# An MLP stage in sweeps of two column groups, with seven block products in place of eight for two token blocks

## The chip, the cores and the metric

One core of one Trainium2 chip runs the whole kernel. The metric is the time of the kernel on the device in microseconds (us), the median of several executions. A trace of one more execution, taken by the hardware profiler, is the source of every row shown. Engines have short names: PE is TensorE (matrix products), PEld its weight loads, DVE is VectorE, ACT is ScalarE, POOL is GpSimd, SP issues the DMAs.

## The reference

```python
attn = linear_attention(q, k, v, omega)          # 4 batches, 8 heads, 576 tokens, head size 64
x = attn.reshape(2304, 512)
xn = x / sqrt(mean(x * x) + 1e-6) * rms_g
x = (silu(xn @ w_gate) * (xn @ w_val)) @ w_out   # 512 -> 1536 -> 512, the GLU stage
out = silu(x @ w_in) @ w_out2                    # 512 -> 2048 -> 512, the MLP stage
```

The weights arrive in 64-bit floats. The result has 2304 x 512 elements in 32-bit floats.

## The kernel before

Tokens lie in five blocks j = 0 to 4 of 512, 512, 512, 512 and 256 tokens. A block's activations `xs[j]` are held with the 512 features in four chunks of 128 partitions, split in two parts, a high part and a low part (what the high part leaves over). Weights are split in the same way. A product of two such operands is three matmuls for each chunk (`PASS`: high by high, high by low, low by high).

The GLU and the MLP stage run in **sweeps**. A sweep holds the weights of a few groups f of 128 hidden columns in SBUF and goes over all blocks with them. The MLP stage has 16 groups, in six sweeps of 3, 3, 3, 3, 2 and 2. Sweeps alternate between two sets of weight slots: side 0 is `w0_0` to `w0_5`, side 1 is `w1_0` to `w1_8`. Slots 0 to 2 of side 1 lie in a pool of their own (`we`). A sweep's input weights "i" come in the first slots, its output weights "p" in the next ones.

For a block j and a group f, `g1_mlp` (L254) makes the input product in an accumulator of tag `g` (12 matmuls through `part`, L226), ACT takes the SiLU (L260) into a tile of tag `s`, and `split_h` (L217) makes the two parts of h: ACT copies the high part (L219), DVE subtracts (L220). When all groups of the sweep are done for a block, `g2_mlp` (L300) makes the output products in accumulators of tag `y`, one for each 128 tokens, with three matmuls a group (L313). DVE adds each into the block's sum `ya[j]` (L324). In the first MLP sweep ACT copies instead (L322), in the last the sums are stored by DMA. Tags `g` and `y` have four accumulators each, `s` has three tiles, `h` four.

`g2_mlp` is a generator. It is put into the program in the middle of the next block's work (`pend`, passed as `mid` or `late`), so that PE has an input product to do while ACT and DVE finish h.

The weights of the next sweep are prepared by `Prep.tick` (L193), which the loop at the end of the kernel (L1031) calls whenever the costs given out by the generators (`yield`, in us of PE) have added up to over 5.5. One tick takes each weight in the pipe a step further: load (DMA of 512 KB), then decode (five DVE operations, L151, L154, L157, L159 and L162, and two POOL additions, L165), then the high part (ACT, L171), then the low part (DVE, L174).

Each engine runs its instructions in the order in which the program writes them. An instruction that waits holds up all that is behind it on its engine.

Of the kernel before, what the change touches and what calls it, by code (L numbers as in the profile page):

```python
# [8 lines left out]
F32 = mybir.dt.float32  # L9
F32R = mybir.dt.float32r  # L10
# [10 lines left out]
def kernel(  # L21
# [14 lines left out]
    nc = tc.nc  # L36
# [48 lines left out]

    ident = const.tile([P, P], F32)
    make_identity(nc, ident)
    bd = const.tile([P, 2, 2 * P], F32R)
    g_sb = const.tile([P, DM], F32)
    mhalf = const.tile([P, 1], F32)  # L90

    xs = [big.tile([P, 2, KC, n], F32R, name=f"xs{j}") for j, n in enumerate(blocks)]
# [9 lines left out]
    sweeps = []  # L102
    f = 0
    for i, n in enumerate([2, 3, 2, 3, 2]):
        sweeps.append((1, list(range(f, f + n)), i % 2))
        f += n
    assert f == NF1
    f = 0
    for i, n in enumerate([3, 3, 3, 3, 2, 2]):
        sweeps.append((2, list(range(f, f + n)), (i + 1) % 2))  # L110
        f += n
    assert f == NF2
    wt = {}

    def wcols(w, f):
# [3 lines left out]
        return w.bitcast(U32)[f * P:(f + 1) * P, :]  # L119

    def prep_list(si):
        kind, fs, side = sweeps[si]
        if kind == 1:
            gv = [e for f in fs for e in (("g", f, wcols(w_gate, f)), ("v", f, wcols(w_val, f)))]
            if si == 0:
                gv.sort(key=lambda e: e[0])
            srcs = gv + [("o", f, wrows(w_out, f)) for f in fs]
        else:
            srcs = [("i", f, wcols(w2_in, f)) for f in fs] + [("p", f, wrows(w2_out, f)) for f in fs]
        return [(side, n, (kind, nm, f), ap) for n, (nm, f, ap) in enumerate(srcs)]  # L130

    class State:
        pass
# [31 lines left out]
            tt(out=mi, in0=mi, in1=(low if step == 5 else high).bitcast(I32), op=ALU.add)  # L165

    def w_high(job, st):
        side, slot, key, ap = job
        pool = pools["w"][2] if side and slot < W_EARLY else pools["w"][side]
        st.t = pool.tile([P, 2, KC * P], F32R, tag=f"w{side}_{slot}", name=f"w{side}_{slot}")  # L170
        nc.scalar.activation(out=st.t[:, 0, :], in_=st.m.bitcast(F32), func=AF.Copy)  # L171

    def w_low(job, st):
# [40 lines left out]
    W_EARLY, GRAIN = 3, 3  # L214
    W_PRIO, F_PRIO = 500.0, 1000.0

    def split_h(s, j):  # L217
        ht = pools["h"][0].tile([P, 2, blocks[j]], F32R, tag="h", name="h", bufs=pools["h"][1])
        nc.scalar.activation(out=ht[:, 0, :], in_=s, func=AF.Copy)  # L219
        nc.vector.tensor_tensor(out=ht[:, 1, :], in0=s, in1=ht[:, 0, :].bitcast(F32), op=ALU.subtract)  # L220
        return ht

    def part(w, j, ps, n0, n1):
        for n in range(n0, n1):
# [29 lines left out]
    def g1_mlp(f, j, hs, mid, late):  # L254
        prep.need((2, "i", f))
        p = ps_tile("ps_g", [P, blocks[j]])
        yield from proj(wt[2, "i", f], j, p)
        yield from late
        s = pools["s"][0].tile([P, blocks[j]], F32, tag="s", name="s", bufs=pools["s"][1])
        nc.scalar.activation(out=s, in_=p, func=AF.Silu)  # L260
        hs[f] = split_h(s, j)
        yield from mid

    def g2_glu(fs, j, hs, first, last):
# [10 lines left out]
        for d in range(KC):  # L275
            ps = ps_tile("ps_y", [P, blocks[j]])
            n = 0
            for f in fs:
                for a, c in PASS:
                    nc.tensor.matmul(  # L280
                        out=ps,
                        lhsT=wt[1, "o", f][:, a, d * P:(d + 1) * P],
                        rhs=hs[f][:, c, :],
                        start=(n == 0),
                        stop=(n == nn - 1),
                    )
                    n += 1
            if first:
                nc.scalar.activation(out=y[:, d, :], in_=ps, func=AF.Copy)
            else:  # L290
                nc.vector.tensor_tensor(out=y[:, d, :], in0=ps, in1=y[:, d, :], op=ALU.add)  # L291
            if last:
                nc.scalar.activation(out=xs[j][:, 0, d, :], in_=y[:, d, :], func=AF.Copy)
                if d:
                    low(d - 1)
            yield nn * blocks[j] / 2365
        if last:
# [32 lines left out]
    n1 = max(i for i, s in enumerate(sweeps) if s[0] == 1)  # L330
    n2 = len(sweeps) - 1

    def stream():
        pend = ()
        prepped = 1
        for si, (kind, fs, side) in enumerate(sweeps):
            for j in range(NB) if si < n2 else [*range(NE), *range(NB - 1, NE - 1, -1)]:
                if si == 0 and j < NE:
                    continue
                hs = {}  # L340
                end = si == n2 and j == NE
                for f in fs:
                    if kind == 1:
# [1 line left out]
                        pend = ()  # L345
                    else:
                        short = blocks[j] < TB * P
                        keep = f == fs[0] and (end or short)
                        mid, late_mid = ((), pend) if short else (pend, ())
                        yield from g1_mlp(f, j, hs, *(((), ()) if keep else (mid, late_mid)))  # L350
                        if not keep:
                            pend = ()
                    if si and prepped == si and si + 1 < len(sweeps):
                        prep.jobs += prep_list(si + 1)
                        prepped += 1
                if kind == 1:
                    pend = g2_glu(fs, j, hs, si == 0, si == n1)
                else:
                    pend = g2_mlp(fs, j, hs, si == n1 + 1, si == n2, end)
        yield from pend  # L360
# [607 lines left out]
    with tc.manual_schedule():  # L968
# [59 lines left out]
        pools["s"] = (late, 3)  # L1028
        prep.jobs += prep_list(1)[W_EARLY:]
        due = 0.0  # L1030
        for c in stream():  # L1031
            due += c
            if due > (W_PACE if prep.done(1) else W_RUSH):
                prep.tick()
# [31 lines left out]
```

## Time and profile before

| what | value |
|---|---|
| time, median of 3 runs | 1016.72 us (1016.62 to 1016.73) |
| time of the profiled execution | 1016.95 us |
| its span | 1015.2 us |
| PE busy | 1006.4 us (99%) |
| DVE busy | 582.5 us (57%) |
| ACT busy | 375.9 us (37%) |
| POOL busy | 282.7 us (28%) |

The span is the time from the first to the last instruction of the program. 1.75 us of the profiled execution lie outside it. Busy shares are means over stages of different kinds; the MLP stage runs from about 610 us to the end.

### The profile page before, as it was taken

The page shows a single profiled execution, that of the slowest core. Times are in us where ns is not written, and L with a number is a line of the kernel's source. Part 1 is how long each engine was busy: PE and PEld are TensorE (multiplying, and loading weights), DVE is VectorE, ACT ScalarE, POOL GpSimd, SP SyncE. Part 2 cuts the span into 40 slices and gives each one's busy share as a digit, 9 for nine tenths or more (in the row PEclk, how much of TensorE's full clock was granted, in tenths as well). Part 3 has the DMA queues.
Part 4 walks back from the last instruction along what each step waited for, and adds up shares of the span by engine and source line. Part 5 has one row for each costly group of instructions (what it writes and reads, how often), then busy time and mean ns, then how long its engine had stood idle before and what let it go on. Part 6 is the DMA issues. An engine that isn't in the chain of part 4 may idle for free.

```text
span 1015.2 us, 14341 instructions
## 1 busy us (share of the span) xinstructions
PE 1006.4 (99%) x5423; PEld 863.5 (85%) x5423; DVE 582.5 (57%) x1289; ACT 375.9 (37%) x861; POOL 282.7 (28%) x287
## 2 busy tenths in 40 slices
PE   8999999999999999999999999999999999999998
PEld 7999998888888888888888888888888888888887
DVE  6899999727852345676332775433654544535633
ACT  6888887344221112222112334443322322322312
POOL 7656653405520013344000331321411312201300
PEclk9999999999999999999999999999999999999999
DMA  7453312202320002232000120210210210200023
GB/s 184 105 151 95 84 43 64 63 21 83 104 62 1 1 1 64 67 98 64 21 1 1 42 63 22 83 42 15 69 42 14 70 43 21 63 1 21 21 84 104
DMA packets 68725, 55.78 MB, mean 55 GB/s; under 512 B 25648, under 2 KB 62768, under 8 KB 68656
## 3 DMA queue, kind: packets, MB, share of 16 engines
q1 hardware_dynamic: 68656, 54.87, 18.4%
q8 instruction: 43, 0.70, 0.3%
q14 instruction: 26, 0.21, 0.1%
HBM read 50.14 MB, written 4.72 MB: 54 GB/s over the span
## 4 chain that ended last, share of the span: by engine, by line
PE 95%; DVE 3%; DMA 1%; SPq 0%; issue 0%; ACT 0%; POOL 0%; DVEq 0%
PE g L226 44%; PE y L313 19%; PE y L280 12%; PE b L590 5%; PE kv L673 3%; PE b L226 3%; PE b L718 3%; PE b L945 2%; PE b L704 2%; PE b L571 1%; PE b L824 1%; DVE w L174 1%; DMA va<-in_v_dram 1%; DVE m L151 0%; DVE raw L154 0%
## 5 line engine op out<-in xcount | busy, mean ns | idle before, releaser
L226 PE MATMUL g<-xs,w 128*128 128x512 f32 (+1 forms) x2256 | 472.8, 368 | 0.0
L226 PEld LDWEIGHTS g<-xs,w 128*128 128x128 f32 x2256 | 391.8, 188 | 74.1
L165 POOL TENSOR_TENSOR m<-m,raw 128x512 int32<-128x512 int32 x136 | 190.6, 1401 | 619.1 <-issue 434.9
L220 DVE TENSOR_TENSOR h<-s,h 128x512 fp32r<-128x512 f32 (+1 forms) x134 | 95.5, 713 | 187.8 <-ACT h L219 187.8
L313 PE MATMUL y<-w,h 128*128 128x512 f32 (+1 forms) x870 | 201.6, 389 | 0.0
L313 PEld LDWEIGHTS y<-w,h 128*128 128x128 f32 x870 | 162.2, 188 | 34.1
L219 ACT ACTIVATE h<-s 128x512 fp32r<-128x512 f32 (+1 forms) x134 | 78.8, 588 | 192.5 <-DVE s L249 170.5
L280 PE MATMUL y<-h,w 128*128 128x512 f32 (+1 forms) x648 | 135.6, 366 | 0.1
L280 PEld LDWEIGHTS y<-h,w 128*128 128x128 f32 x648 | 112.1, 189 | 20.5 <-DVE w L174 0.5
L260 ACT ACTIVATE s<-g 128x512 f32<-128x512 f32 (+1 forms) x80 | 44.5, 556 | 174.5 <-PE g L226 174.3
L324 DVE TENSOR_TENSOR ya<-y,ya 128x512 f32<-128x512 f32 (+1 forms) x91 | 62.3, 684 | 58.6 <-PE y L313 57.5
L249 DVE TENSOR_TENSOR s<-s,g 128x512 f32<-128x512 f32 (+1 forms) x54 | 33.9, 627 | 90.1 <-PE g L226 90.1
L291 DVE TENSOR_TENSOR ya<-y,ya 128x512 f32<-128x512 f32 (+1 forms) x80 | 50.3, 635 | 55.1 <-PE y L280 54.8
L629 ACT ACTIVATE e<-b,nb 128x128 f32<-128x128 f32 x272 | 77.5, 386 | 9.0 <-DVE nb L618 8.6
L171 ACT ACTIVATE w<-m 128x512 fp32r<-128x512 f32 x68 | 42.7, 628 | 100.8 <-POOL m L165 100.7
L590 PE MATMUL b<-bd,hl 128*128 128x256 f32 x432 | 69.3, 297 | 0.3 <-DVE hl L580 0.2
L590 PEld LDWEIGHTS b<-bd,hl 128*128 128x128 f32 x432 | 56.4, 191 | 1.8 <-DVE hl L580 0.8
L243 ACT ACTIVATE s<-g 128x512 f32<-128x512 f32 (+1 forms) x54 | 29.7, 550 | 65.9 <-PE g L226 65.7
L174 DVE TENSOR_TENSOR w<-m,w 128x512 fp32r<-128x512 f32 x68 | 51.5, 758 | 4.1 <-ACT w L171 3.8
L605 DVE TENSOR_REDUCE small<-b 128x4 f32<-128x512 f32 x72 | 50.1, 696 | 5.9 <-PE b L590 3.3
L530 POOL TENSOR_TENSOR sq<-x 128x512 f32<-128x512 f32 (+1 forms) x40 | 39.4, 987 | 33.5 <-DVE rd L744 7.3
L534 POOL TENSOR_TENSOR sq<-sq 128x256 f32<-128x256 f32 (+2 forms) x80 | 44.7, 569 | 3.3
(69 smaller groups left out, 781.7 us busy)
## 6 DMA issues: line engine op xcount, KB each, us to landing
raw<-in_moe_w_out_dram SPq DMA_DIRECT2D x28, 512.0 KB, 3.5
raw<-in_moe_w_in_dram SPq DMA_DIRECT2D x16, 512.0 KB, 3.6
raw<-in_moe_w_gate_dram SPq DMA_DIRECT2D x12, 512.0 KB, 3.5
raw<-in_moe_w_val_dram SPq DMA_DIRECT2D x12, 512.0 KB, 3.5
x<-in_k_dram SPq DMA_DIRECT2D x16, 256.0 KB, 3.4
va<-in_v_dram SPq DMA_DIRECT2D x32, 128.0 KB, 3.4
x<-in_q_dram SPq DMA_DIRECT2D x16, 256.0 KB, 3.1
out_dram<-ya SPq DMA_DIRECT2D x15, 256.0 KB, 2.0
```

The costliest lines, as they stand in the source:

```text
L165: tt(out=mi, in0=mi, in1=(low if step == 5 else high).bitcast(I32), op=ALU.add)
L174: nc.vector.tensor_tensor(out=st.t[:, 1, :], in0=st.m.bitcast(F32), in1=st.t[:, 0, :].bitcast(F32), op=ALU.subtract)
L219: nc.scalar.activation(out=ht[:, 0, :], in_=s, func=AF.Copy)
L220: nc.vector.tensor_tensor(out=ht[:, 1, :], in0=s, in1=ht[:, 0, :].bitcast(F32), op=ALU.subtract)
L226: nc.tensor.matmul(out=ps, lhsT=w[:, a, cc * P:(cc + 1) * P], rhs=xs[j][:, c, cc, :], start=(n == 0), stop=(n == 3 * KC - 1),)
L280: nc.tensor.matmul(out=ps, lhsT=wt[1, "o", f][:, a, d * P:(d + 1) * P], rhs=hs[f][:, c, :], start=(n == 0), stop=(n == nn - 1),)
L291: nc.vector.tensor_tensor(out=y[:, d, :], in0=ps, in1=y[:, d, :], op=ALU.add)
L313: nc.tensor.matmul(out=ps, lhsT=hs[f][:, a, t * P:(t + 1) * P], rhs=wt[2, "p", f][:, c, d0:d1], start=(n == 0), stop=(n == nn - 1),)
L324: nc.vector.tensor_tensor(out=o[:, t, d0:d1], in0=ps, in1=o[:, t, d0:d1], op=ALU.add)
L590: nc.tensor.matmul(out=st.ps[:, 2 * j:2 * j + 2, :].rearrange("p h m -> p (h m)"), lhsT=st.hl[:, c, j, :], rhs=bd[:, a, :], start=(n == 0) ...
L605: nc.vector.tensor_reduce(out=st.mx, in_=st.ps, axis=AX.X, op=ALU.max)
L629: nc.scalar.activation(out=st.e[:, h, :], in_=st.ps[:, h, :], func=AF.Exp, bias=st.nb[:, h:h + 1])
```

## The change

The MLP stage gets eight sweeps of two groups. Token blocks 0 and 1 (`PAIR`) are worked on together, at the end of each sweep's blocks (after block 2 in the last sweep). Their input products for the two groups form a product of 2 by 2 block matrices: two groups by two halves of the 512 features, times two halves of the features by two token blocks. `pair_products` makes it with seven block products in place of eight, by sums of the operands: S1 to S4 of the weights (S for sums, made once a sweep by `weight_sums` on DVE and ACT, in slots 4 and 5 of side 0) and T1 to T4 of the activations (made once, by `t_jobs`, in slots 4 to 9 of side 1 and, T4, over the first half of `xs[1]`). Results are put together by DVE from the accumulators. The small jobs of both are written into the program one step for each `yield` (`along`). The output products of the pair (`both`, 48 matmuls) are written behind the first input product of the next sweep.

`split_h` can leave its subtraction to a later `settle`. `bd` and `g_sb` move to a pool that is closed after the attention stage, which makes room for the tenth slot of side 1. In the last GLU sweep the first half of `xs[1]` is no longer written.

```diff
--- before.py
+++ after.py
@@ -85,8 +85,8 @@
 
     ident = const.tile([P, P], F32)
     make_identity(nc, ident)
-    bd = const.tile([P, 2, 2 * P], F32R)
-    g_sb = const.tile([P, DM], F32)
+    bd = load_p.tile([P, 2, 2 * P], F32R, tag="bd", name="bd")
+    g_sb = load_p.tile([P, DM], F32, tag="g_sb", name="g_sb")
     mhalf = const.tile([P, 1], F32)
 
     xs = [big.tile([P, 2, KC, n], F32R, name=f"xs{j}") for j, n in enumerate(blocks)]
@@ -102,14 +102,13 @@
     sweeps = []
     f = 0
     for i, n in enumerate([2, 3, 2, 3, 2]):
-        sweeps.append((1, list(range(f, f + n)), i % 2))
+        sweeps.append((1, list(range(f, f + n)), [(i % 2, k) for k in range(3 * n)]))
         f += n
     assert f == NF1
-    f = 0
-    for i, n in enumerate([3, 3, 3, 3, 2, 2]):
-        sweeps.append((2, list(range(f, f + n)), (i + 1) % 2))
-        f += n
-    assert f == NF2
+    for f in range(0, NF2, 2):
+        sweeps.append((2, [f, f + 1], [(1 - f // 2 % 2, k) for k in range(4)]))
+    T_SLOTS, S_SLOTS = [(1, k) for k in range(4, 10)], [(0, 4), (0, 5)]
+    assert NF2 % 2 == 0
     wt = {}
 
     def wcols(w, f):
@@ -119,7 +118,7 @@
         return w.bitcast(U32)[f * P:(f + 1) * P, :]
 
     def prep_list(si):
-        kind, fs, side = sweeps[si]
+        kind, fs, slots = sweeps[si]
         if kind == 1:
             gv = [e for f in fs for e in (("g", f, wcols(w_gate, f)), ("v", f, wcols(w_val, f)))]
             if si == 0:
@@ -127,7 +126,11 @@
             srcs = gv + [("o", f, wrows(w_out, f)) for f in fs]
         else:
             srcs = [("i", f, wcols(w2_in, f)) for f in fs] + [("p", f, wrows(w2_out, f)) for f in fs]
-        return [(side, n, (kind, nm, f), ap) for n, (nm, f, ap) in enumerate(srcs)]
+        return [(*slot, (kind, nm, f), ap) for slot, (nm, f, ap) in zip(slots, srcs)]
+    def w_tile(side, slot):
+        pool = pools["w"][2] if side and slot < W_EARLY else pools["w"][side]
+        return pool.tile([P, 2, KC * P], F32R, tag=f"w{side}_{slot}", name=f"w{side}_{slot}")
 
     class State:
         pass
@@ -165,9 +168,7 @@
             tt(out=mi, in0=mi, in1=(low if step == 5 else high).bitcast(I32), op=ALU.add)
 
     def w_high(job, st):
-        side, slot, key, ap = job
-        pool = pools["w"][2] if side and slot < W_EARLY else pools["w"][side]
-        st.t = pool.tile([P, 2, KC * P], F32R, tag=f"w{side}_{slot}", name=f"w{side}_{slot}")
+        st.t = w_tile(*job[0:2])
         nc.scalar.activation(out=st.t[:, 0, :], in_=st.m.bitcast(F32), func=AF.Copy)
 
     def w_low(job, st):
@@ -214,11 +215,25 @@
     W_EARLY, GRAIN = 3, 3
     W_PRIO, F_PRIO = 500.0, 1000.0
 
-    def split_h(s, j):
+    owed = []
+    def split_h(s, j, defer=False):
         ht = pools["h"][0].tile([P, 2, blocks[j]], F32R, tag="h", name="h", bufs=pools["h"][1])
         nc.scalar.activation(out=ht[:, 0, :], in_=s, func=AF.Copy)
-        nc.vector.tensor_tensor(out=ht[:, 1, :], in0=s, in1=ht[:, 0, :].bitcast(F32), op=ALU.subtract)
+        owed.append(lambda: dsub(ht[:, 1, :], s, ht[:, 0, :].bitcast(F32)))
+        if not defer:
+            settle()
         return ht
+    def settle():
+        while owed:
+            owed.pop(0)()
+    def dsub(out, a, b):
+        nc.vector.tensor_tensor(out=out, in0=a, in1=b, op=ALU.subtract)
+    def dadd(out, a, b):
+        nc.vector.tensor_tensor(out=out, in0=a, in1=b, op=ALU.add)
 
     def part(w, j, ps, n0, n1):
         for n in range(n0, n1):
@@ -255,6 +270,7 @@
         prep.need((2, "i", f))
         p = ps_tile("ps_g", [P, blocks[j]])
         yield from proj(wt[2, "i", f], j, p)
+        settle()
         yield from late
         s = pools["s"][0].tile([P, blocks[j]], F32, tag="s", name="s", bufs=pools["s"][1])
         nc.scalar.activation(out=s, in_=p, func=AF.Silu)
@@ -289,9 +305,9 @@
                 nc.scalar.activation(out=y[:, d, :], in_=ps, func=AF.Copy)
             else:
                 nc.vector.tensor_tensor(out=y[:, d, :], in0=ps, in1=y[:, d, :], op=ALU.add)
-            if last:
+            if last and d >= last[0]:
                 nc.scalar.activation(out=xs[j][:, 0, d, :], in_=y[:, d, :], func=AF.Copy)
-                if d:
+                if d > last[0]:
                     low(d - 1)
             yield nn * blocks[j] / 2365
         if last:
@@ -330,14 +346,208 @@
     n1 = max(i for i, s in enumerate(sweeps) if s[0] == 1)
     n2 = len(sweeps) - 1
 
+    PAIR = (0, 1)
+    HALF = KC * P // 2
+    LHS = {"A11": (0, 0), "A12": (0, 1), "A22": (1, 1), "S1": (2, 0), "S2": (2, 1), "S3": (3, 0), "S4": (3, 1)}
+    RHS = {"B11": (0, 0), "B21": (0, 1), "B22": (1, 1), "T4": (1, 0)}
+    sw, tw, todo = {}, {}, []
+    def rhs(nm, k):
+        if nm in RHS:
+            j, h = RHS[nm]
+            return xs[PAIR[j]][:, :, 2 * h + k, :]
+        return tw[nm, k]
+    def s_tile():
+        return pools["s"][0].tile([P, TB * P], F32, tag="s", name="s", bufs=pools["s"][1])
+    def split(out, value):
+        def high():
+            nc.scalar.activation(out=out()[:, 0, :], in_=value(), func=AF.Copy)
+        return [high, lambda: dsub(out()[:, 1, :], value(), out()[:, 0, :].bitcast(F32))]
+    def weight_sums(fs):
+        lo, hi = slice(0, HALF), slice(HALF, 2 * HALF)
+        v = {}
+        def w(f, c):
+            return wt[2, "i", f][:, c, :].bitcast(F32)
+        def first():
+            prep.need(*[(2, "i", f) for f in fs])
+            settle()
+            v[0], v[1] = s_tile(), s_tile()
+            b, c, s, u = w(fs[1], 0), w(fs[1], 1), v[0], v[1]
+            dadd(s[:, lo], b[:, lo], b[:, hi])
+            dadd(u[:, lo], c[:, lo], c[:, hi])
+            dadd(s[:, lo], s[:, lo], u[:, lo])
+        def second():
+            dsub(v[0][:, hi], v[0][:, lo], w(fs[0], 0)[:, lo])
+            dsub(v[0][:, hi], v[0][:, hi], w(fs[0], 1)[:, lo])
+            dsub(v[1][:, hi], w(fs[0], 0)[:, hi], v[0][:, hi])
+        def third():
+            dadd(v[1][:, hi], v[1][:, hi], w(fs[0], 1)[:, hi])
+            dsub(v[1][:, lo], w(fs[0], 0)[:, lo], w(fs[1], 0)[:, lo])
+            dadd(v[1][:, lo], v[1][:, lo], w(fs[0], 1)[:, lo])
+        def fourth():
+            dsub(v[1][:, lo], v[1][:, lo], w(fs[1], 1)[:, lo])
+            sw[fs[0]] = [w_tile(*slot) for slot in S_SLOTS]
+        p, q = [split(lambda n=n: sw[fs[0]][n], lambda n=n: v[n]) for n in range(2)]
+        return [[first], [second], [third], [fourth, p[0]], [p[1], q[0]], [q[1]]]
+    def t_jobs():
+        jobs = []
+        for k in range(2):
+            def b(r, c, k=k):
+                return ya[PAIR[c - 1]].rearrange("p (c t) -> p c t", c=KC)[:, 2 * r - 2 + k, :]
+            v = {}
+            def first(k=k, v=v, b=b):
+                v[0], v[1] = s_tile(), s_tile()
+                dsub(v[0], b(1, 2), b(1, 1))
+            def out(n, k=k):
+                if n == 3:
+                    return rhs("T4", k)
+                if ("T%d" % (n + 1), k) not in tw:
+                    tw["T%d" % (n + 1), k] = w_tile(*T_SLOTS[2 * n + k])
+                return tw["T%d" % (n + 1), k]
+            parts = [split(lambda n=n, out=out: out(n), lambda n=n, v=v: v[n % 2]) for n in range(4)]
+            jobs += [
+                [first], [parts[0][0], lambda v=v, b=b: dsub(v[1], b(2, 2), v[0])], [parts[1][0], parts[0][1]],
+                [parts[1][1]], [lambda v=v, b=b: dsub(v[0], b(2, 2), b(1, 2))],
+                [parts[2][0], lambda v=v, b=b: dsub(v[1], b(2, 1), v[1])], [parts[3][0], parts[2][1]], [parts[3][1]],
+            ]
+        return jobs
+    def pair_products(fs, hs, pend):
+        cost = 6 * TB * P / 2365
+        prep.need(*[(2, "i", f) for f in fs])
+        flush()
+        t = [wt[2, "i", f] for f in fs] + sw[fs[0]]
+        def product(a, b, ps, start, stop):
+            n, h = LHS[a]
+            for m, (w, c) in enumerate(PASS):
+                for k in range(2):
+                    o = h * HALF + k * P
+                    nc.tensor.matmul(
+                        out=ps,
+                        lhsT=t[n][:, w, o:o + P],
+                        rhs=rhs(b, k)[:, c, :],
+                        start=start and m == 0 and k == 0,
+                        stop=stop and m == 2 and k == 1,
+                        skip_group_check=True,
+                    )
+        def silu(out, in_):
+            nc.scalar.activation(out=out, in_=in_, func=AF.Silu)
+        (f0, f1), (j0, j1) = fs, PAIR
+        hs[j0], hs[j1] = {}, {}
+        a = ps_tile("ps_g", [P, TB * P])
+        product("A11", "B11", a, True, True)
+        y = s_tile()
+        nc.scalar.activation(out=y, in_=a, func=AF.Copy)
+        settle()
+        yield cost
+        b = ps_tile("ps_g", [P, TB * P])
+        product("S2", "T2", b, True, True)
+        dadd(y, y, b)
+        yield cost
+        c = ps_tile("ps_g", [P, TB * P])
+        product("S3", "T3", c, True, True)
+        z = s_tile()
+        dadd(z, y, c)
+        yield cost
+        e = ps_tile("ps_g", [P, TB * P])
+        product("S1", "T1", e, True, True)
+        dadd(z, z, e)
+        silu(z, z)
+        yield cost
+        yield from pend
+        product("A12", "B21", a, False, True)
+        u = s_tile()
+        silu(u, a)
+        hs[j0][f0] = split_h(u, j0, True)
+        yield cost
+        product("A22", "T4", c, False, True)
+        settle()
+        v = s_tile()
+        dadd(v, y, c)
+        silu(v, v)
+        hs[j0][f1] = split_h(v, j0, True)
+        yield cost
+        product("S4", "B22", e, False, True)
+        dadd(y, y, e)
+        silu(y, y)
+        settle()
+        hs[j1][f0] = split_h(y, j1, True)
+        hs[j1][f1] = split_h(z, j1, True)
+        yield cost
+    def flush():
+        while todo:
+            for job in todo.pop(0):
+                job()
+    def along(gen):
+        for c in gen:
+            yield c
+            if todo:
+                for job in todo.pop(0):
+                    job()
     def stream():
         pend = ()
         prepped = 1
-        for si, (kind, fs, side) in enumerate(sweeps):
-            for j in range(NB) if si < n2 else [*range(NE), *range(NB - 1, NE - 1, -1)]:
+        for si, (kind, fs, _) in enumerate(sweeps):
+            def more(si=si):
+                nonlocal prepped
+                if si and prepped == si and si + 1 < len(sweeps):
+                    prep.jobs += prep_list(si + 1)
+                    prepped += 1
+            js = [*range(NB)]
+            if kind == 2:
+                js = [j for j in js if j not in PAIR]
+                js = js + [PAIR] if si < n2 else [2, PAIR, NB - 1, NE]
+            after_pair = si > n1 + 1
+            if after_pair:
+                todo.extend(weight_sums(fs))
+            for n, j in enumerate(js):
                 if si == 0 and j < NE:
                     continue
                 hs = {}
+                if j == PAIR:
+                    yield from pair_products(fs, hs, pend)
+                    def both(fs=fs, si=si, hs=hs):
+                        for j in PAIR:
+                            yield from g2_mlp(fs, j, hs[j], si == n1 + 1, si == n2, False)
+                    pend = both()
+                    after_pair = True
+                    continue
                 end = si == n2 and j == NE
                 for f in fs:
                     if kind == 1:
@@ -345,16 +555,20 @@
                         pend = ()
                     else:
                         short = blocks[j] < TB * P
-                        keep = f == fs[0] and (end or short)
-                        mid, late_mid = ((), pend) if short else (pend, ())
+                        keep = f == fs[0] and (end or short) and not after_pair
+                        mid, late_mid = ((), pend) if short or after_pair else (pend, ())
                         yield from g1_mlp(f, j, hs, *(((), ()) if keep else (mid, late_mid)))
                         if not keep:
                             pend = ()
-                    if si and prepped == si and si + 1 < len(sweeps):
-                        prep.jobs += prep_list(si + 1)
-                        prepped += 1
+                        after_pair = False
+                    more()
+                    if kind == 1 and si == n1 and j == PAIR[1] + 1 and f == fs[0]:
+                        todo.extend(t_jobs())
+                    if si == n1 + 1 and n == 0 and f == fs[0]:
+                        todo.extend(weight_sums(fs))
                 if kind == 1:
-                    pend = g2_glu(fs, j, hs, si == 0, si == n1)
+                    last = ((KC // 2,) if j == PAIR[1] else (0,)) if si == n1 else ()
+                    pend = g2_glu(fs, j, hs, si == 0, last)
                 else:
                     pend = g2_mlp(fs, j, hs, si == n1 + 1, si == n2, end)
         yield from pend
@@ -1028,7 +1242,7 @@
         pools["s"] = (late, 3)
         prep.jobs += prep_list(1)[W_EARLY:]
         due = 0.0
-        for c in stream():
+        for c in along(stream()):
             due += c
             if due > (W_PACE if prep.done(1) else W_RUSH):
                 prep.tick()
```

## Rows read from the trace of the kernel before

**Rows 1.** The page: its span, busy time by engine, and the granted clock by slice.
```profile
span 1015.2 us, 14341 instructions
...
PE 1006.4 (99%) x5423; PEld 863.5 (85%) x5423; DVE 582.5 (57%) x1289; ACT 375.9 (37%) x861; POOL 282.7 (28%) x287
...
PEclk9999999999999999999999999999999999999999
```

**Rows 2.** Groups by form, 616 to 1016 us: busy us, mean ns | idle before.
```profile
L313 PE MATMUL y<-w,h 128*128 128x512 f32 x858 | 200.1, 390 | 0.0
...
L324 DVE TENSOR_TENSOR ya<-y,ya 128x512 f32<-128x512 f32 x89 | 61.4, 690 | 58.3 <-PE y L313 57.3
```

**Rows 3.** The chain that ended last, 600 to 1016 us: start us, us, what.
```profile
651.29 8.40 PE g L226 x36
659.69 8.19 PE y L313 x36
...
709.05 8.16 PE g L226 x36
717.21 8.16 PE y L313 x36
...
931.69 5.58 PE y L313 x24
...
976.01 5.44 PE g L226 x24
```

**Rows 4.** Timeline of DVE, 794 to 797 us: start us, us, instruction.
```profile
794.21 0.68 DVE L174 TENSOR_TENSOR w<-m,w 128x512 fp32r<-128x512 f32 x1
794.93 0.43 DVE L151 TENSOR_SCALAR m<-raw 128x512 uint32<-128x512 uint32 x1
...
796.62 0.68 DVE L324 TENSOR_TENSOR ya<-y,ya 128x512 f32<-128x512 f32 x1
```

**Rows 5.** Timeline of DVE, 432 to 435 us, operations on 256 columns.
```profile
432.83 1.08 DVE L291 TENSOR_TENSOR ya<-y,ya 128x256 f32<-128x256 f32 x3
```

**Rows 6.** Timeline of DVE at 41 us, where the second reads the first.
```profile
41.13 0.16 DVE L611 SCALAR_TENSOR_TENSOR small<-ns,small 128x4 f32<-128x4 f32 x1
41.33 0.16 DVE L618 SCALAR_TENSOR_TENSOR nb<-ns,small 128x4 f32<-128x4 f32 x1
```

**Rows 7.** Timeline of ACT and DVE, 976 to 981 us.
```profile
976.04 0.69 DVE L324 TENSOR_TENSOR ya<-y,ya 128x512 f32<-128x512 f32 x1 [0.67 <-PE y L313]
978.76 0.60 ACT L260 ACTIVATE s<-g 128x512 f32<-128x512 f32 x1 [6.90 <-PE g L226]
979.39 0.63 ACT L219 ACTIVATE h<-s 128x512 fp32r<-128x512 f32 x1
980.06 0.69 DVE L220 TENSOR_TENSOR h<-s,h 128x512 fp32r<-128x512 f32 x1 [3.32 <-ACT h L219]
```

**Rows 8.** Timeline of POOL and DVE, 853 to 864 us.
```profile
853.87 2.68 POOL L165 TENSOR_TENSOR m<-m,raw 128x512 int32<-128x512 int32 x2 [33.67 <-issue]
855.44 0.69 DVE L324 TENSOR_TENSOR ya<-y,ya 128x512 f32<-128x512 f32 x1 [1.11 <-PE y L313]
...
859.99 2.70 POOL L165 TENSOR_TENSOR m<-m,raw 128x512 int32<-128x512 int32 x2 [3.44 <-issue]
...
861.50 1.73 DVE L220 TENSOR_TENSOR h<-s,h 128x512 fp32r<-128x512 f32 x1 [1.65 <-ACT h L219]
```

**Rows 9.** Timeline of POOL and DVE, 660 to 665 us.
```profile
660.89 0.42 DVE L162 TENSOR_SCALAR m<-m 128x512 uint32<-128x512 uint32 x1
661.23 0.69 DVE L220 TENSOR_TENSOR h<-s,h 128x512 fp32r<-128x512 f32 x1
661.45 3.68 POOL L165 TENSOR_TENSOR m<-m,raw 128x512 int32<-128x512 int32 x2 [6.59 <-DVE m L162]
...
661.83 0.69 DVE L174 TENSOR_TENSOR w<-m,w 128x512 fp32r<-128x512 f32 x1
662.55 1.42 DVE L151 TENSOR_SCALAR m<-raw 128x512 uint32<-128x512 uint32 x1
...
663.89 1.53 DVE L154 TENSOR_SCALAR raw<-raw 128x512 uint32<-128x512 uint32 x1
```

**Rows 10.** The page: DMA issues of the MLP weights, KB each, us to landing.
```profile
raw<-in_moe_w_out_dram SPq DMA_DIRECT2D x28, 512.0 KB, 3.5
raw<-in_moe_w_in_dram SPq DMA_DIRECT2D x16, 512.0 KB, 3.6
```

## The prediction

> **What bounds the kernel now.** I read the page first. PE is busy for 1006.4 of 1015.2 us, at the full granted clock in every slice (2.4 GHz, the upper of its two levels) [rows 1]. The groups of the MLP stage then show no idle time before an output product, while DVE idles 57 us for PE before the additions of L324 [rows 2]. So PE sets the end, and what matters is PE's time from one instruction to the next. The mean durations can't be used for that: the matmuls overlap. The chain that ended last gives it, as each piece there ends where the next begins: 36 input matmuls in 8.16 us in a sweep on side 0, 0.2267 us each, and in 8.40 us on side 1, 0.2333 us each [rows 3]. The reader is to see two things: fewer matmuls shorten the kernel at once, and so much DVE work may be added as does not make PE wait, no more.
>
> **What PE saves.** Per sweep, blocks 0 and 1 need 2 blocks x 2 groups x 12 = 48 input matmuls; seven products of 6 are 42. On side 0 that saves 6 x 0.2267 = 1.36 us. On side 1 the slow pace goes with weights in slots 0 to 2; S1 to S4 lie on side 0, so three products run at 0.2333 and four at 0.2267: 48 x 0.2333 - 18 x 0.2333 - 24 x 0.2267 = 1.56 us. Four sweeps each: 11.7 us. The output matmuls stay 864, but in a sweep of two on side 1 their weights lie in slots 2 and 3: 5.58 us for 24, 0.2325 each, against 8.19 for 36, 0.2275, in a sweep of three [rows 3]. So 18 tiles x 18 matmuls x 0.0050 = 1.6 us come back. Net -10.1 us.
>
> **What DVE gets.** Prices first. An operation on 512 columns lasts 0.69 us, the next one starts 0.60 after it [rows 9]; one on 256 columns 0.42 and 0.33 [rows 5]. If an operation reads the result of the one just before it, there is no overlap: the next starts 0.04 after the end [rows 6], which makes 0.46 for 256 columns. A decode is 1.69 us from its first start to the next instruction [rows 4], and then two POOL additions of 1.3 [rows 8]. SiLU to low part is 1.30 us from start to start, and both engines begin 0.03 to 0.1 behind PE [rows 3, 7].
>
> New on DVE in a sweep: ten sums of 256 columns in four steps (W1 to W4), two low parts, five sums in the pair. Eight sweeps in place of six also mean 36 more additions of 0.60. Over a sweep of 48 us (216 full matmuls less 6, at 0.227) all this fits. The question is the place: W1 to W3 are written between the pair's output tiles, each ahead of the addition of a tile, and `y` has four accumulators. The fifth tile of the pair can't start before the first has been added, and so on to the eighth, which waits for the fourth.
>
> Adding up the costs that the generators yield shows what else is written there. Ticks come every 6.5 us at the same places in every sweep: after the fourth product, after the seventh (low part of one weight, decode of another), and after the third output tile (a low part).
>
> Now the queue of DVE, with time 0 at the end of the seventh product. PE goes on with block 2's input product to 2.72 and output tiles of 1.36; the fifth would start at 8.16, the eighth at 12.24. The tick after the fourth product keeps POOL busy until -0.9; the low part of u, ready at -1.4, waits for that, then v is summed, and SiLU and split put v's low part at 1.6. The tick: low part from 2.2, decode from 3.0 to 4.65. Then `settle`: low parts of y and z at 4.65 and 5.26; then W1, its first two sums at 5.87 and 6.2.
>
> Here POOL comes in. While it works, a DVE operation with both inputs in SBUF waits: L220 took 1.73 us from the middle of POOL's additions, where L324, with one input in PSUM, took 0.69 as ever [rows 8]. If DVE runs without a gap, POOL waits: it started behind L220 and L174 and took 3.68 for two additions, and then L151 and L154 each waited for one [rows 9]. The Trainium skill says the same ("SBUF — State Buffer", section "Who interferes with whom"): a DVE instruction with two SBUF inputs contends with a GpSimd instruction that reads SBUF, and the second to issue blocks until the first is done. By that rule this placement is bad, since all the ten sums have two SBUF inputs; the trace agrees with 1.73 against 0.69.
>
> So, as in [rows 9], POOL gets in at the first gap, W1's third sum, which reads the second: POOL from 6.5 to 7.8, the sum done at 8.1, POOL's second addition until 9.25. The first tile's addition (PSUM) runs at 8.0 to 8.7. W2's three sums, each reading the one before, wait for POOL and end at 9.5, 9.95 and 10.45; second addition to 11.05; W3 to 12.1; third addition to 12.8; low part of the tick to 13.4; W4; fourth addition to 14.35. PE: fifth tile at 8.75, sixth at 11.1, seventh at 12.85, eighth at 14.4 in place of 12.24. That is 2.15 us late, and about 2.0 after the slower pace of side 1, by which PE would have come later anyway (4 of 7 pairs). There are seven such boundaries, 14.0 us. In the first of them ACT copies in place of DVE's additions, but the copy of the fourth tile stands behind the split of the first sum tile, which waits for W4: about the same.
>
> Bounds for a boundary: 0, if POOL never holds DVE (then v's low part comes 0.4 earlier, and the fourth addition ends at 12.4), and 2.65, if POOL's first addition goes right behind the low part of y (fourth addition at 15.05). I take the order of [rows 9], which is the nearest: decode, two low parts and POOL, as here.
>
> **What costs nothing, and what hides it.** T1 to T4: eight differences and eight low parts, 9.6 us of DVE over some 35 us of the last GLU sweep; its `y` groups leave some 8 us of input products between them, so a late addition is caught up. With that cover gone it would cost 2 to 3 us once. `s`: W holds two of three tiles for five output tiles, in which no SiLU needs one. `h`: the pair holds all four; the next split waits for block 0's output tiles, and its reader comes 8 us later. Weights of a sweep: ready one tick before W1 reads them, loads land in 3.5 us [rows 10], under one tick. `bd`, `g_sb` and their pool: the same bytes elsewhere. In the last sweep nothing stands ahead of v's low part: wanted at 2.6, there at about 2.0.
>
> **Sum.** 1016.95 - 11.7 + 1.6 + 14.0 = 1020.85 us for a profiled execution. The median of the runs shown is 0.23 below it: 1020.6 us, 0.4% slower.
>
> **Rivals.**
> *DVE keeps up, no stall*: 1016.72 - 10.1 = 1006.6 us, on the other side. For it: DVE idles 57 us for PE in this stage [rows 2], and the walk has margins of a few tenths. Against it: the last 12 us of DVE's queue ahead of the fourth addition are packed. It decides at a boundary's price under 1.44 us (10.1 / 7).
> *POOL holds DVE only once*: its second addition falls wholly under the tile's addition, W2 doesn't wait (0.75 less), 1.2 us a boundary: 8.4, so 1015.0 us, no change that counts.
> *Strict turns*: POOL right behind the low part of y, 2.65 x 7 = 18.6, so 1025.2 us. The first-issued-first reading of the same page would give this. Against it: in [rows 9] POOL asked 0.2 us into L220 and L174 still went before it.
>
> **Chances.** A change of over 0.2% (2 us) is about what this measurement can tell from none. Forecast (2.0 a boundary) 0.46, strict turns 0.13, so slower 0.59; held once, or another near balance, 0.16; no stall or little, 0.25. The range runs from 1008 to 1027: it leaves out half of the no-stall case below and a stall of over 2.9 us a boundary above. The forecast's own range is 1018.8 to 1023.
>
> **What would show it.** In the trace after: 48 matmuls fewer with `g` as output; PE idle only in seven groups, each in the pair's output tiles of blocks 0 and 1, tiles five to eight, released by DVE's addition (in the first by ACT's copy), about 2 us together; sums of 256 columns that took 1 us or more in place of 0.42 beside POOL's additions; the decode between the seventh product and W1. The saving is right if the pair's products are 42 matmuls at 0.227 to 0.231 us with no gap. I am wrong if PE is idle at other places (the accumulators `g`, the split of v), if T's jobs stall the last GLU sweep, or if the fourth addition ends before 12.2 us.

## The result and the profile after

The changed kernel takes 1026.87 us (median of four runs, 1025.82 to 1027.75), the kernel before 1016.67 beside it: ratio 1.010, 95% interval 1.0083 to 1.0118. It is 10.2 us slower, and the interval lies clear of 1. The profiled execution took 1027.2 us.

The page and the waits of PE, after; they answer to [rows 1] and [rows 2].

```profile
span 1025.4 us, 14468 instructions
...
PE 1004.3 (98%) x5375; PEld 854.1 (83%) x5375; DVE 694.0 (68%) x1475; ACT 389.9 (38%) x891; POOL 282.1 (28%) x287
```
```profile
engine line waited for: us in total, times, longest us
PE y L329 <- DVE ya L340: 11.6, 6, 2.1
```

48 matmuls fewer, as counted, and a wait that was not there: PE before output products, for DVE's additions (L340 is L324 of before), six times. How large the loss is, the chain that ended last shows, read from one piece to the next:

```profile
653.75 2.72 PE g L241 x12
656.48 11.18 PE y L329 x48
667.65 5.46 PE g L241 x24
...
689.62 5.44 PE g L452 x24
695.05 2.72 PE y L329 x12
...
767.87 3.19 PE y L329 x12
771.06 5.45 PE g L241 x24
```

L452 are the pair's products: the first four of the seven, 24 matmuls, take 5.44 us, 0.2267 each, with no gap. A **boundary** is the pair's 48 output matmuls (eight tiles) behind the first input product of the next sweep. There are seven. At the first, where ACT copies the tiles, they take 11.18 us. At the other six DVE adds them. The timeline of the second of these six:

```profile
754.07 2.89 PE L241 MATMUL g<-xs,w 128*128 128x512 f32 x12
...
755.97 0.69 DVE L233 TENSOR_TENSOR h<-s,h 128x512 fp32r<-128x512 f32 x1 [0.63 <-ACT h L222]
756.58 0.69 DVE L175 TENSOR_TENSOR w<-m,w 128x512 fp32r<-128x512 f32 x1
756.79 5.76 PE L329 MATMUL y<-w,h 128*128 128x512 f32 x24
757.30 0.43 DVE L154 TENSOR_SCALAR m<-raw 128x512 uint32<-128x512 uint32 x1
...
758.98 2.40 DVE L233 TENSOR_TENSOR h<-s,h 128x512 fp32r<-128x512 f32 x2
759.20 3.35 POOL L168 TENSOR_TENSOR m<-m,raw 128x512 int32<-128x512 int32 x2 [6.00 <-issue]
761.31 1.86 DVE L236 TENSOR_TENSOR s<-w 128x256 f32<-128x256 f32 x2
...
763.55 0.68 DVE L340 TENSOR_TENSOR ya<-y,ya 128x512 f32<-128x512 f32 x1
...
764.38 6.68 PE L329 MATMUL y<-w,h 128*128 128x512 f32 x24 [1.83 <-DVE ya L340]
...
768.66 0.68 DVE L340 TENSOR_TENSOR ya<-y,ya 128x512 f32<-128x512 f32 x1
...
770.90 4.48 PE L241 MATMUL g<-xs,w 128*128 128x512 f32 x19
```

The reader is to see the order on DVE: low part of v, the tick (L175, decode from L154), the low parts of y and z (L233, 2.40 us for two), the sums of W1 (L236, 1.86 us for two of 256 columns), and only then the first addition, at 763.55. PE had finished the fourth tile by 762.55 (756.79 + 5.76) and starts the fifth at 764.38. The 48 matmuls take 770.90 - 756.79 = 14.11 us here. Read so at all six: 14.79, 14.11, 14.19, 14.12, 14.20 and 14.10. Without a wait, as in the runs below, they take 10.91 on side 0 and 11.18 on side 1: 85.5 - 3 x 10.91 - 3 x 11.18 = 19.2 us lost. The 11.6 us in the list of waits are those ahead of the fifth tiles; the rest was lost at tiles six to eight.

The last GLU sweep lost as well. Its first piece and the first piece of the MLP stage in the chain, before and after:

```profile
544.11 10.91 PE g L226 x48
618.13 7.00 PE g L226 x30
```
```profile
543.37 10.91 PE g L241 x48
618.96 5.60 PE g L241 x24
```

It took 618.13 - 544.11 = 74.02 us before and 75.59 us after. So in this execution: -10.1 (as forecast) + 19.2 + 1.6 = 10.7, of 10.25 measured. The stages up to 544 us were 0.7 us shorter, which was not followed up; 0.3 us are then not accounted for.

### The profile page after: what moved, and what is told of

The parts are those of the page before. It is cut to its first block, busy times and chain, and to the rows that moved or that the text cites. A ratio compares the mean times of both kernels' runs of the same rounds, so it can differ in the third digit from the quotient of the medians.

```text
span 1025.4 us, 14468 instructions
## 1 busy us (share of the span) xinstructions
PE 1004.3 (98%) x5375; PEld 854.1 (83%) x5375; DVE 694.0 (68%) x1475; ACT 389.9 (38%) x891; POOL 282.1 (28%) x287
## 4 chain that ended last, share of the span: by engine, by line
PE 85%; DVE 12%; ACT 2%; issue 1%; DMA 0%; SPq 0%; ACTq 0%; DVEq 0%
PE g L241 32%; PE y L329 15%; PE y L296 12%; PE g L452 6%; PE b L804 5%; PE b L241 3%; PE kv L887 3%; PE b L932 2%; DVE h L233 2%; DVE s L236 2%; PE b L1159 2%; PE b L785 2%; PE b L918 1%; DVE s L233 1%; ACT h L222 1%
## 5 line engine op out<-in xcount | busy, mean ns | idle before, releaser
L241 PE MATMUL g<-xs,w 128*128 128x512 f32 (+1 forms) x1872 | 383.4, 363 | 0.0
L241 PEld LDWEIGHTS g<-xs,w 128*128 128x128 f32 x1872 | 319.7, 188 | 58.3
L329 PE MATMUL y<-w,h 128*128 128x512 f32 (+1 forms) x870 | 210.3, 395 | 12.7 <-DVE ya L340 11.6
L233 DVE TENSOR_TENSOR h<-s,h 128x512 fp32r<-128x512 f32 (+1 forms) x134 | 109.3, 825 | 99.6 <-ACT h L222 99.6
L222 ACT ACTIVATE h<-s 128x512 fp32r<-128x512 f32 (+1 forms) x134 | 77.9, 587 | 170.1 <-DVE s L264 165.1
L340 DVE TENSOR_TENSOR ya<-y,ya 128x512 f32<-128x512 f32 (+1 forms) x127 | 85.0, 682 | 31.5 <-PE y L329 30.9
L307 DVE TENSOR_TENSOR ya<-y,ya 128x512 f32<-128x512 f32 (+1 forms) x80 | 50.3, 635 | 56.1 <-PE y L296 55.9
L276 ACT ACTIVATE s<-g 128x512 f32<-128x512 f32 (+1 forms) x48 | 25.0, 521 | 87.6 <-PE g L241 87.3
L258 ACT ACTIVATE s<-g 128x512 f32<-128x512 f32 (+1 forms) x54 | 29.6, 549 | 65.5 <-PE g L241 64.9
L175 DVE TENSOR_TENSOR w<-m,w 128x512 fp32r<-128x512 f32 x68 | 50.3, 740 | 4.1 <-ACT w L172 3.8
L452 PE MATMUL g<-xs,w 128*128 128x512 f32 x192 | 46.7, 392 | 0.0
```

What stands on the lines that cost most here:

```text
L175: nc.vector.tensor_tensor(out=st.t[:, 1, :], in0=st.m.bitcast(F32), in1=st.t[:, 0, :].bitcast(F32), op=ALU.subtract)
L233: nc.vector.tensor_tensor(out=out, in0=a, in1=b, op=ALU.subtract)
L241: nc.tensor.matmul(out=ps, lhsT=w[:, a, cc * P:(cc + 1) * P], rhs=xs[j][:, c, cc, :], start=(n == 0), stop=(n == 3 * KC - 1),)
L329: nc.tensor.matmul(out=ps, lhsT=hs[f][:, a, t * P:(t + 1) * P], rhs=wt[2, "p", f][:, c, d0:d1], start=(n == 0), stop=(n == nn - 1),)
L340: nc.vector.tensor_tensor(out=o[:, t, d0:d1], in0=ps, in1=o[:, t, d0:d1], op=ALU.add)
L452: nc.tensor.matmul(out=ps, lhsT=t[n][:, w, o:o + P], rhs=rhs(b, k)[:, c, :], start=start and m == 0 and k == 0, stop=stop and m == 2 and k ...
```

## The experiments

**Sums written later.** In the changed kernel the sums of a boundary stand ahead of its additions from the second MLP sweep on; here they come behind, except in the last sweep.

```diff
-            if after_pair:
+            if after_pair and si == n2:
                 todo.extend(weight_sums(fs))
...
-                    if si == n1 + 1 and n == 0 and f == fs[0]:
+                    if n1 < si < n2 and n == 0 and f == fs[0]:
                         todo.extend(weight_sums(fs))
```

> The ten sums of a sweep are written behind the pair's output tiles, from the second group of block 2 on; in the last sweep alone they stay where they were. Theory (the stall is a matter of place: W1 to W3 stand ahead of the additions that free the accumulators y): the six boundaries at which PE waits for DVE cost about 3.0 us each in the trace of the changed kernel, five of them go, 1026.9 - 15 = 1012 us, and PE waits for DVE at one boundary only. Rival (DVE has too much to do in a sweep, wherever it stands): the waits turn up at other places and the time stays over 1022 us.

1011.59 us, ratio 0.9951 (0.9937 to 0.9966). The waits of PE, and the same boundary in the chain:

```profile
PE y L329 <- DVE ya L340: 1.8, 1, 1.8
```
```profile
750.45 2.72 PE g L241 x12
753.17 11.18 PE y L329 x48
764.35 5.46 PE g L241 x24
```

11.18 us in place of 14.11: DVE had the time, in another place. The rival falls.

**POOL's additions left out** for one weight of a sweep.

```diff
-                    for s in range(7):
+                    for s in range(5 if late else 7):
                         w_decode(job, st, s, n)
```

Here `late` holds for the second output weight of each MLP sweep after the first. Its fifth decode step shifts by 0 bits instead of 3, at the same length.

> The two POOL additions are left out for the one weight of each sweep that is decoded between the seventh product and W1, so its values are wrong; DVE's operations stay. Theory (POOL holds DVE's operations with two SBUF inputs there): low parts and W1 run without a wait, the fifth output tile starts on time, and what is left is a wait of about 1 us over tiles six to eight in place of 3.0: 6 x 1.9 less, about 1015 us. Rival (the sums' own length makes the stall, POOL does not matter): 1025 to 1027 us.

1013.42 us, ratio 0.997 (0.9959 to 0.9981). DVE's timeline at the same boundary:

```profile
756.53 1.29 DVE L234 TENSOR_TENSOR h<-s,h 128x512 fp32r<-128x512 f32 x2
757.74 0.75 DVE L237 TENSOR_TENSOR s<-w 128x256 f32<-128x256 f32 x2
758.53 0.42 DVE L237 TENSOR_TENSOR s<-s 128x256 f32<-128x256 f32 x1
758.87 0.69 DVE L341 TENSOR_TENSOR ya<-y,ya 128x512 f32<-128x512 f32 x1
```

The same operations as in the rows above take 1.29 in place of 2.40 us and 0.75 in place of 1.86: two waits of 1.1 us for POOL. The 48 matmuls take 11.99 us on side 0 and 11.90 on side 1, so 5.4 of the 19.2 us are left. With the sums where they are, POOL's hold makes 2.3 us of a boundary's 3.2, a little more than the 1.9 expected.

**Two ticks a product earlier**, nothing left out.

```diff
         settle()
-        yield cost
+        yield 2 * cost
...
         hs[j1][f1] = split_h(z, j1, True)
-        yield cost
+        yield 0.0
```

> The changed kernel with one number moved: the first product yields twice its cost and the seventh none, so two ticks of a sweep are written after the third and the sixth product in place of the fourth and the seventh. Nothing is left out, and W1 to W3 stay ahead of the additions. Theory (POOL's additions beside the low parts of y and z and W1 make most of the stall): POOL is done when W1 comes, W1's first sum takes 0.42 us, the stall falls from 3.0 to about 1.4 us a boundary, 1016 to 1018 us. Rival (the number of operations ahead of the additions alone sets it): as the changed kernel, 1025 us or more.

1018.54 us, ratio 1.0021 (1.0012 to 1.003). W1 runs free, but the low parts of v, y and z now meet POOL:

```profile
755.46 0.68 DVE L236 TENSOR_TENSOR s<-s,g 128x512 f32<-128x512 f32 x1
...
755.67 3.04 POOL L168 TENSOR_TENSOR m<-m,raw 128x512 int32<-128x512 int32 x2 [5.00 <-ACT w L172]
756.05 3.81 DVE L233 TENSOR_TENSOR h<-s,h 128x512 fp32r<-128x512 f32 x3
...
757.60 10.61 PE L329 MATMUL y<-w,h 128*128 128x512 f32 x42 [0.66 <-DVE h L233]
```

PE waits 0.66 us for v's low part, now at all seven boundaries, and loses another 0.8 to 1.1 at the later tiles of six. Those six lose 1.5 to 1.7 us each, a little over the 1.4 expected, and the first loses 0.9: so the time lies 0.5 us above the expected 1016 to 1018. The place of two ticks is worth 8 us.

**Sweeps of two alone**, in the kernel before.

```diff
-    for i, n in enumerate([3, 3, 3, 3, 2, 2]):
+    for i, n in enumerate([2] * 8):
```

> The kernel before with the MLP stage in eight sweeps of two groups and nothing else. Theory: only the slower output products of side 1 count, +1.6 us, 1018.3 us; the 36 additions more on DVE are hidden. Rival (sweeps of two cost by themselves, by weights that come late or additions that PE waits for): 1022 us or more.

1018.25 us, ratio 1.0017 (1.0007 to 1.0027): +1.75 us beside its own runs of before (1016.5). The chain of its first MLP sweep, on side 1, has the pace taken for it in the prediction, 5.58 us for 24 output matmuls:

```profile
634.70 5.58 PE y L313 x24
```

**The ten sums left out.** S1 to S4 are split from weights as they are, so only the time is of use.

```diff
-            v[0], v[1] = s_tile(), s_tile()
-            b, c, s, u = w(fs[1], 0), w(fs[1], 1), v[0], v[1]
-            dadd(s[:, lo], b[:, lo], b[:, hi])
+            v[0], v[1] = w(fs[0], 0), w(fs[1], 0)
...
```

> The changed kernel without the ten sums of each sweep: S1 to S4 are split straight from two weights, so the result is not the reference's; products, splits and everything else stay. Theory: the first addition follows the low parts of y and z and no tile waits, so the whole saving of the seven products shows: 1016.7 - 10.1 = 1006.6 us, up to 1009 with what the last GLU sweep lost. Rival (the products save less than counted, or the pair's own chain costs): 1012 us or more.

1008.04 us, ratio 0.9918 (0.9903 to 0.9933). No wait for an addition is left; with the 1.6 us of the GLU sweep taken off, 1006.4: the saving of the products, net of the sweeps of two, is 10 us, as counted. POOL's additions are all still there, and the low parts of y and z still take 2.40 us, but the 48 matmuls take 10.91 to 11.18 us: the hold costs PE nothing when the sums do not stand behind it.

**The last sweep too**, on top of the sums written later. Its blocks go 2, 4, the pair, 3.

```diff
-            if after_pair and si == n2:
-                todo.extend(weight_sums(fs))
...
-                js = js + [PAIR] if si < n2 else [2, PAIR, NB - 1, NE]
+                js = js + [PAIR] if si < n2 else [2, NB - 1, PAIR, NE]
...
+                after_pair = after_pair and not end
...
-                    if n1 < si < n2 and n == 0 and f == fs[0]:
+                    if si > n1 and n == 0 and f == fs[0]:
```

> As the kernel with the sums written later, and the last sweep too: its blocks go 2, 4, the pair, 3, so that its sums have room behind the pair's output tiles. Theory: the one boundary that was left with a wait of about 3 us loses it, 1011.6 - 3.0 = 1008.6 us, and PE waits for no addition of L340 at all. Rival (the stall moves: the last sweep's pair now waits for its sums, or the end gets longer): 1010.5 us or more.

1012.15 us (1011.17 to 1012.63), ratio 0.9954 (0.9942 to 0.9967): a miss, the rival is right. The old wait is gone, a new one came:

```profile
991.17 0.63 ACT L222 ACTIVATE h<-s 128x512 fp32r<-128x512 f32 x1 [6.56 <-PE y L329]
...
992.99 0.69 DVE L233 TENSOR_TENSOR h<-s,h 128x512 fp32r<-128x512 f32 x1 [0.46 <-ACT h L222]
993.59 2.48 DVE L340 TENSOR_TENSOR ya<-y,ya 128x512 f32<-128x512 f32 x4
994.31 1.53 SPq L343 DMA_DIRECT2D out_dram<-ya  x3
994.43 2.05 PE L329 MATMUL y<-w,h 128*128 128x512 f32 x4 [2.67 <-DVE ya L340]
```

Block 3's first split (L222, at 991.17) waits for a tile of `h` that block 0's output products hold. The low parts of its two splits stand on DVE ahead of the additions, so PE waits 2.67 us: the same trap, four accumulators and something ahead of the first addition.

**T's jobs spread**, on top of that one.

```diff
-                        todo.extend(t_jobs())
+                        jobs = t_jobs()
+                        todo.extend(x for job in jobs[:8] for x in (job, []))
+                        todo.extend(jobs[8:])
```

> As the one with the last sweep's sums moved, and the second half of T's jobs written into the first MLP sweep, the first half at every second step. Theory (T's jobs, one a step, made PE wait 1.3 us in the last GLU sweep, at 604 and 616 us of the changed kernel's trace): 1.3 us less, 1007.3 us, with no wait of PE for h in that sweep. Rival (those waits come from elsewhere in that sweep, or T's jobs cost as much in the first MLP sweep): no change to the kernel sent with it, within 0.5 us.

1011.09 us (1009.7 to 1011.72), ratio 0.9944 (0.9932 to 0.9957). The expected 1007.3 us was missed, because it was reckoned from the 1008.6 us that the run before it had missed; against that run it is 1.06 us less, of 1.3 expected. The times of the two overlap, so the trace decides. The ends of the last GLU sweep in the chain:

```profile
543.65 10.91 PE g L241 x48
617.67 5.60 PE g L241 x24
```

That is 74.02 us, as before the change, and PE no longer waits for h there: T's jobs had cost 1.6 us. The wait of 2.7 us of the run before it is still there.

**Block 3's splits apart**, on top of both.

```diff
+                        half = end and after_pair
+                        if half:
+                            late_mid = islice(pend, TB)
...
-                        if not keep:
+                        if not keep and not half:
```

with the line that cleared `after_pair` in the last sweep taken out again.

> As the kernel with T's jobs spread, with one thing moved in the last sweep: block 3's first split is written behind block 0's four output tiles and its second ahead of block 1's four, in place of both ahead of all eight. Theory (DVE's low part of block 3's first h waited for a tile of h that block 0's output tiles held, and the additions stood behind it, 2.8 us of PE at 993 us): that wait goes and the halved clock that followed it in some runs, 1011.1 - 2.9 = 1008.2 us, down to 1007 us. Rival (the last sweep's order costs by itself, at its end): 1010 us or more.

1006.52 us (1006.07 to 1006.58), ratio 0.99 (0.9884 to 0.9917): 0.5 us under the expected 1007 to 1008.2, 1% faster than the kernel before, and 20 us faster than the change as it was made. PE's waits in its trace are those of the first 20 us:

```profile
PE b L1197 <- DMA om<-in_omega_dram: 2.8, 1, 2.8
PE b L789 <- DMA x<-in_k_dram: 1.0, 1, 1.0
PE kv L891 <- DMA va<-in_v_dram: 0.5, 1, 0.5
PE b L808 <- DVE hl L798: 0.2, 1, 0.2
```

## Why the prediction was right, and by how much it was off

The direction was right, and so were the place of the stall and its cause, DVE's queue ahead of the additions. The loss was set too low: 3.9 us forecast, 10.2 measured. The 1026.87 us lie above the forecast's own range (1018.8 to 1023) and only 0.13 us inside the whole one (1008 to 1027). That the number fell inside is luck: one term was too small, one too large and one missing, and a mean granted clock that fell in some executions, told of at the end, moves the time by more than that margin.

*The saving.* Right: 10.1 us counted; without stalls the products and the sweeps of two give 1006.52 against 1016.45, 9.9 us. Sweeps of two by themselves: +1.6 counted, +1.75 measured.

*The stall.* At the fifth to eighth tiles of the pair, released by DVE's additions, as said. Mis-sized: 7 x 2.0 = 14.0 forecast, 6 x 3.2 = 19.2 measured. Two terms are off, in opposite ways.

The step that failed is the order of POOL and DVE, taken from [rows 9], where POOL waited for two DVE operations in a row. Here POOL's first addition went between the low parts of y and z, its second between z's low part and W1: 2.40 and 1.86 us for two operations each, at all six boundaries the same. That is the order of the rival of strict turns, which had a chance of 0.13. It had put the fourth addition's end at 15.05 us after the seventh product; it ended at 769.34, 15.3 us after PE's next matmul began at 754.07 (14.35 in the forecast). A boundary cost 3.2 us, against 2.65 by that rival and 2.0 by the forecast. Of the 0.55 us over the rival's price, 0.2 is the later end of the fourth addition, and 0.1 the restart of the eighth tile (its second matmul began 0.34 us after its first, in place of 0.23); 0.1 on the mean of six is the clock at one boundary, told of below. The rest is not accounted for.

The trace of the kernel before had more than [rows 9] to go by. Five times a POOL addition came up during L220 with another operation with two SBUF inputs right behind it on DVE. At 661.45 it waited for both. At 251.10, 256.62, 262.14 and 953.12 it went between the two. The second addition of this POOL row is the one at 256.62, and L174 takes 1.79 us in place of 0.69:

```profile
255.23 3.02 POOL L165 TENSOR_TENSOR m<-m,raw 128x512 int32<-128x512 int32 x2 [2.49 <-DVE m L162]
...
256.40 0.69 DVE L220 TENSOR_TENSOR h<-s,h 128x512 fp32r<-128x512 f32 x1 [0.70 <-ACT h L219]
257.01 1.79 DVE L174 TENSOR_TENSOR w<-m,w 128x512 fp32r<-128x512 f32 x1
```

So the row that looked nearest was the exception in that trace, and strict turns were the common case.

The other term is the first boundary, where ACT copies. I let it cost as much as the others. It cost nothing: 48 matmuls in 11.18 us. The forecast had the fourth copy behind a split that waits for W4. It did stand behind that split (L376), but the split reads only the first sum tile, which W2 completes (W4 finishes the other one):

```profile
664.12 0.63 ACT L376 ACTIVATE w<-s 128x512 fp32r<-128x512 f32 x1 [1.36 <-DVE s L233]
...
664.65 0.58 ACT L338 ACTIVATE ya<-y 128x512 f32<-128x512 f32 x1
```

The copy was done at 665.23, and the eighth tile was due at 656.48 + 7/8 of 11.18 = 666.3.

*T's jobs.* Costed at nothing, hidden by the gaps between `y` groups; they cost 1.6 us. This was one of the signs given for being wrong ("if T's jobs stall the last GLU sweep"), and it came. The low parts of `xs`, the splits of h and the decode stand in the same 35 us on DVE; the price given for a lost cover, 2 to 3 us, is what it came near.

*The rivals.* "DVE keeps up" gave 1006.6 us, which is what the last experiment measures (1006.52) once nothing stands ahead of the additions; in the change as made, a boundary's price was 3.2 us against the 1.44 from which it decides. "POOL holds DVE only once" is out: two holds a boundary are in the rows. What the Trainium skill states of a GpSimd instruction that reads SBUF and a DVE instruction with two SBUF inputs ("SBUF — State Buffer", section "Who interferes with whom"), that they contend, is borne out: DVE's operations were held for 1.1 us twice a boundary, and leaving POOL's additions out was worth 13.8 of 19.2 us.

Left open: why [rows 9] have POOL behind two DVE operations, where four other places of the same trace, and all six boundaries after, have strict turns.

## What to carry to other kernels

Work off the critical path is not hidden because an engine has idle time over the stage; it is hidden if nothing that PE will need stands behind it in that engine's queue. With n accumulators, ask for each insertion what stands ahead of the addition that frees the next one, and walk the queue from there. The same seven products were worth +10 us as first written and -10 us with their small operations in other places; moving the ten sums alone made 15 of these 20 us. The price of a DVE operation with two SBUF inputs has to be taken together with what POOL does at that moment. And before one row of a trace is made the rule for the order of two engines, look for every other place where the two meet.

## What the runs showed of the hardware

After one of the waits the clock of TensorE fell. The windows of 4 us behind the first and the second DVE boundary's wait, after (busy us of PE, PEld, DVE, ACT and POOL, each with its count; then PEclk, the share of the DMA engines and GB/s):

```profile
712.00:716.00 4.00, 3.84 (x10) 3.06 (x11) 3.90 (x10) 0.63 (x1) 0.00 (x0) 0.57 0.33 114
764.00:768.00 4.00, 3.43 (x13) 2.23 (x14) 3.90 (x10) 0.63 (x1) 0.00 (x0) 1.00 0.37 122
```

The mean granted clock is 0.57 of 2.4 GHz in the first, so the lower level, 1.2 GHz, in most of it, and 1.00 in the second. PE's matmuls had been 2.4 and 2.2 us apart just before; two more gaps of 2.4 us, which ended at 815 and 918 us, were followed by the full clock. In the run with the last sweep too, 0.60 followed a gap of 3.1 us:

```profile
994.00:998.00 4.00, 3.57 (x10) 2.91 (x11) 2.71 (x5) 0.00 (x0) 0.00 (x0) 0.60 0.71 262
```

In the profiled execution with T's jobs spread, a gap of the same 3.06 us was followed by the full clock, so the length of the gap alone does not decide it. That execution took 1009.7 us; the other four of that kernel, with a mean granted clock of 0.998 in place of 1.000, took 1011.01 to 1011.72. Of the changed kernel, too, the execution at 1.000 took 1025.82 us and the three at 0.998 took 1026.54 to 1027.75.

The prediction had no term for it. At the first DVE boundary it cost 0.6 us (14.79 against 14.19 and 14.20 at the other two on side 0). PE had no further gap at tiles six to eight there, as it had at the boundaries with the full clock, so part of the slower time would have been spent waiting for additions.
